# Sums of an attention through DRAM: one write and four reads of 256-byte runs, or two writes and four reads of 1024- and 1280-byte runs, in a new order of the instructions

## Chip, cores and metric

The kernel runs on one core of one Trainium2 chip. Its time is the device time of one execution in microseconds (us). A run's profile comes from one execution that the hardware profiler recorded, whose own device time is given beside the span from its first to its last instruction.

## What is computed

Causal attention with a decay, and on its result a gated projection. Eight batches, eight heads, 576 positions, 64 numbers a head:

```python
scores = q @ k.T / sqrt(64) + cum[:, None] - cum[None, :]      # cum: running sum of log(clip(f))
scores = where(j > i, -1e9, scores); scores -= scores.max(-1)
attn = exp(scores); attn = attn / (attn.sum(-1) + 1e-9)
x = attn @ v                                                   # heads side by side: 8 x 576 x 512
gate = sigmoid(sum_k conv_w[k] * x[position - 4 + k])          # five taps
out = (gate * (x @ w_val)) @ w_out
```

Inputs and outputs are float32, the weights of the projections are float64 and are decoded on the chip into two parts each.

## The kernel before

The 64 heads are worked off as 32 pairs, numbered i (four pairs to a batch). One pair's way through the engines:

- **Scores** (`plan_s`). The 576 queries are nine blocks of 64. In three groups (`SG`) TensorE multiplies keys with queries in quarters of the array and adds the decay by a product of a selector `pk` with a table `st` in bfloat16 (for pair 0, by a float32 product of `p1` with the running sum). VectorE adds the mask and takes the extreme (line 421), ScalarE takes the exponential and, beside it, the sum of each row into `zs` (line 425).
- **Transposes** (`plan_pt`). VectorE transposes the exponentials in 32 by 32 blocks into `T` (line 460). ScalarE or GpSimd copies half of `T` into `U`, and four DMAs (U copies, "U<-T") bring the other halves across partitions. U has two buffers.
- **Sums.** GpSimd or VectorE adds 1e-9 into `zr` (line 433), VectorE takes reciprocals and transposes them (lines 437 and 438) into `zt`: row 32a + b of it holds, for block b, the 32 numbers of part a (a = 0..3; parts 0 and 1 are one half of the partitions, 2 and 3 the other). One DMA writes them to a DRAM buffer `zd` of 128 x 32 (four buffers), and four DMAs read them back into `zb`, each to 64 partitions that all get the same numbers: one for each side (five or four blocks, `SIDES`) and half.
- **Product** (`plan_pv`). TensorE multiplies U with v ("U,vt"), in 54 small products. VectorE multiplies the result by `zb` into `x32` (line 517).
- **Gate and projections** (`plan_pv`, `plan_moe`). x is split in two parts, `xh` and `xl`, for fp32r products. The five taps run on ScalarE, GpSimd and VectorE; for the first two pairs (`NCV`) they run on TensorE instead, with diagonal matrices that line 534 makes ("x,tm"). After every fourth pair the batch goes through `Mv` (x by w_val), the gate (line 593), a split in `hh` and `hl`, `Mo` (by w_out), an eviction (lines 634 and 636) and a store.

At the start VectorE, ScalarE and GpSimd also decode the weights (`plan_w`, lines 693 to 709; `sh`, `sl`, `ot` are its buffers), and `split` makes the table `st`: three casts to bfloat16 with two subtractions between them (line 347).

**What sets the order.** No loop order is followed. `Plan.add` records each step with its dependences; `ORDER` is a compressed table of numbers that says which step comes next, on which of the engines that may do it, and which PSUM bank its result gets. `Plan.order` unpacks it. Every engine and the DMA queue of SyncE (SP), which issues nearly all transfers, then run their steps strictly in that order, and a step that waits holds what stands behind it on its engine.

```python
def load(cls, span, prio, out, in_, reads=(), writes=(), hold=0.57, early=False):
    return plan.add(cls, {"SP": hold, "ACT": hold} if early else {"SP": hold}, prio,
                    lambda e: (nc.sync if e == "SP" else nc.scalar).dma_start(out=out, in_=in_), reads, writes, dma=span)
```

`hold` and `span` are the planner's costs; the chip does not see them.

Of the kernel before, what the change touches and what calls it, by code (L numbers as in the profile page):

```python
# [15 lines left out]
P = 128  # L16
D = 64
S = 576
PAD = 64
W = PAD + S  # L20
NB = 4
L0 = NB * P
# [22 lines left out]
    "c-l>pc}!G!w#Vz<y0!0n)vf*3erw<N?beRI1kjfN`bSgpk_Pz$kVzDsL`o-7WD=mA1ZZB;(EcIlB!G4T=p+s8OB&=Qio8USKN@rrK_>y^4?$k?prmKstyKNaId#tGd(Q"  # L45
    "b?8V<ls;V$4bI4Q0lH;#LU<KZkgC+;qYgEn!yI1mWoD1Zl8CM*(~aILs=xD;*xJiu`Q7(f6N2tXaU5^fG00m)DTx{XT{Frb1E1d6~YSPK+@Zr~aTfw)iw)B!a?Ca4PPf"
    "%>5{xKp@lLLJl!H3D^ndgwmx2iyo$B+Nn6U?<cCO+t+X2_z=Epm}H-8il?k_Tb(V+DXkM7ZD?#0hXXkz;oP>gbrW=C=i3hJ$!`Xp}Zr!0}k<RM1)vPT!;1`h+rcAf};^"
    "iL@og&?h^WlH-I<L6seZj3*06S0y6-GxKEe`28hGJ6{3vr5jup(<XfaiV3D{)nj<|29snz(c@md6LYxOjiI0eHaBqmOz&_Fd2_bKgc1c|F2x)`pA};|Z@;>P%NlVxy-K"
    "4h=EQAQbLy(Xo;3DxEagA_|{s!nEbP-AfkQ^jaz)fJ3be-~o@{za;>;qTHT(FnWMH!<EQYtBvq&kWO9Hu-aE)!2v_-u%Tkq?P`L^^4L(n~3kU*Yhe21G$OxJ8+v)Kd!N"
    "CdvV2meNgL1uMWL*h*;v?-Qm76ND;omas|zs5_K(%3JUZnN3PjQ>4?(^W-$;A(_r@CO43W$nE4b^DeoAvOuW^TftxH{d9x`lTebAbQKgc&Vf{_gt|eWr0>!Z#t0o_R8U"  # L50
    "=vP5M54lnyeM=+pE$dXQ0Im>AWJ?+G8ld*riJ3S))NqlQUoyq4;r=1Jq^8qy9}MY2#i_!;sXd4YU~u}&_5Fn)=A0B(}i_-~k8#vAhglAD;dj1FcGbB5W+_(TRNt<2w;T"
    "g*=8EOUohPim${sOPEeR4R+Zx=b~)8>nlXF6IGqf!Rf+QOtNA<qinoC6t#;fHlY*W76;?Y9AG2PcR3l!^|@*7aL|3*dx@>)Jj@C<35{B3(#EnpQvHHhO)$-W3Mu6XkuC"
# [92 lines left out]
def tile_decay_attention_gated_mlp(  # L145
# [11 lines left out]
    B, H = out.shape[0], out.shape[2] // D  # L157
# [635 lines left out]
```

## Time and profile before

| | |
|---|---|
| median of 3 runs | 438.51 us (438.19 to 442.37) |
| the profiled execution | 437.04 us |
| its span, first to last instruction | 435.3 us |
| mean granted TensorE clock in it | 0.991 |

Busy times in a profile are unions of an engine's instructions. "PE" is TensorE's matmuls, "PEld" its weight loads, DVE VectorE, ACT ScalarE, POOL GpSimd, SP SyncE. In a list of waits or behind "<-" stands what released the waiting instruction last: an engine with tile and line, or a DMA. PEclk is the granted share of the full clock.

### The profile page before, as it was taken

The page shows a single profiled execution, that of the slowest core. Times are in us where ns is not written, and L with a number is a line of the kernel's source. Part 1 is how long each engine was busy: PE and PEld are TensorE (multiplying, and loading weights), DVE is VectorE, ACT ScalarE, POOL GpSimd, SP SyncE. Part 2 cuts the span into 40 slices and gives each one's busy share as a digit, 9 for nine tenths or more (in the row PEclk, how much of TensorE's full clock was granted, in tenths as well). Part 3 has the DMA queues.
Part 4 walks back from the last instruction along what each step waited for, and adds up shares of the span by engine and source line. Part 5 has one row for each costly group of instructions (what it writes and reads, how often), then busy time and mean ns, then how long its engine had stood idle before and what let it go on. Part 6 is the DMA issues. An engine that isn't in the chain of part 4 may idle for free.

```text
span 435.3 us, 16742 instructions
## 1 busy us (share of the span) xinstructions
PE 416.7 (96%) x6660; PEld 356.1 (82%) x6660; DVE 373.7 (86%) x1034; ACT 338.1 (78%) x840; POOL 287.9 (66%) x295
## 2 busy tenths in 40 slices
PE   7679899999999989999999999999999999999996
PEld 5456678888998878888898889887898888988885
DVE  6999889998999888898899987978999987997751
ACT  7899879998888869888777877667987988763430
POOL 4575847587959692898779475898675779752200
PEclk9899999999999999999999999999999999999999
DMA  7889987878777975977885677777867776387112
GB/s 286 291 213 240 239 233 196 223 206 210 216 202 199 253 199 152 256 211 200 220 249 143 184 212 206 197 209 216 243 174 209 223 184 191 74 205 224 57 46 98
DMA packets 74694, 86.93 MB, mean 200 GB/s; under 512 B 48120, under 2 KB 48120, under 8 KB 74616
## 3 DMA queue, kind: packets, MB, share of 16 engines
q1 hardware_dynamic: 74328, 85.28, 71.1%
q8 instruction: 52, 0.85, 0.8%
q10 hardware_dynamic: 288, 0.59, 0.4%
q14 instruction: 26, 0.21, 0.2%
HBM read 51.99 MB, written 10.26 MB: 143 GB/s over the span
## 4 chain that ended last, share of the span: by engine, by line
PE 88%; DVE 4%; DMA 3%; ACT 2%; issue 1%; POOL 1%; SPq 0%; POOLq 0%
PE banks L235 88%; DVE banks L421 2%; DMA U<-T 1%; DMA vt<-in_v_dram 1%; DVE T L460 1%; ACT P L425 1%; DMA cwu<-in_conv_w_dram 1%; POOL wall L709 1%; DVE negm L421 0%; ACT L334 0%; SPq L262 0%; POOL U L250 0%; DVE sh L707 0%; ACT sl L693 0%; ACT gate L333 0%
## 5 line engine op out<-in xcount | busy, mean ns | idle before, releaser
L425 ACT ACTIVATE P<-banks,negm 128x576 f32<-128x576 f32 (+8 forms) x288 | 150.0, 530 | 42.4 <-DVE negm L421 30.7
L421 DVE CUSTOM_DVE_ANT_0 banks<-banks,mk 128x576 f32<-128x576 f32 (+8 forms) x288 | 135.3, 508 | 15.2 <-PE banks L235 11.4
L562 POOL TENSOR_TENSOR gate<-gate,tm 128x576 f32<-128x576 f32 x77 | 109.7, 1425 | 33.6 <-DVE gate L560 12.0
L460 DVE STREAM_TRANSPOSE T<-P 128x1088 f32<-128x1088 f32 (+2 forms) x96 | 110.5, 1165 | 5.2 <-ACT P L425 2.8
L235 PE MATMUL banks<-xh,wall 128*128 128x288 f32 x512 | 107.1, 298 | 0.0
L235 PE MATMUL banks<-Xr 64*64 64x288 f32 (+8 forms) x1280 | 103.1, 410 | 1.4 <-DMA Xr<-in_x_dram 1.4
L235 PEld LDWEIGHTS banks<-U,vt 64*64 64x64 f32 x3456 | 91.8, 135 | 8.3 <-issue 3.1
L235 PE MATMUL banks<-U,vt 64*64 64x128 f32 (+1 forms) x3456 | 93.2, 256 | 3.8 <-issue 1.8
L235 PE MATMUL banks<-wall,hh 128*128 128x512 f32 x288 | 90.4, 395 | 0.0
L235 PEld LDWEIGHTS banks<-xh,wall 128*128 128x128 f32 x512 | 83.3, 188 | 4.2 <-issue 1.4
L235 PEld LDWEIGHTS banks<-Xr 64*64 64x64 f32 x1280 | 63.8, 134 | 16.5 <-issue 5.9
L235 PE MATMUL banks<-xl,wall 128*128 128x288 f32 x256 | 75.4, 295 | 0.0
L235 PEld LDWEIGHTS banks<-wall,hh 128*128 128x128 f32 x288 | 52.6, 188 | 13.0 <-issue 1.6
L425 ACT ACTIVATION_READ_ACCUMULATOR P<-banks,negm 128x1 f32 x288 | 58.7, 204 | 0.0
L250 ACT COPY U<-T 128x1440 f32<-128x1440 f32 x40 | 55.5, 1396 | 3.4 <-DVE T L460 1.7
L235 PE MATMUL banks<-wall,hl 128*128 128x512 f32 x144 | 56.2, 390 | 0.0
L235 PE MATMUL banks<-st,pk 64*64 64x448 bf16 (+8 forms) x620 | 45.8, 291 | 7.5 <-ACT st L250 3.7
L257 POOL TENSOR_SCALAR tm<-x,cw 128x576 f32<-128x576 f32 x40 | 30.1, 753 | 34.1 <-DVE gate L560 13.3
L235 PEld LDWEIGHTS banks<-xl,wall 128*128 128x128 f32 x256 | 48.0, 188 | 0.3
L607 POOL TENSOR_TENSOR hl<-h,hh 128x576 fp32r<-128x576 f32 (+2 forms) x34 | 34.4, 1027 | 12.6 <-DVE gate L560 4.1
L526 POOL TENSOR_TENSOR xl<-x,xh 128x576 fp32r<-128x576 f32 x25 | 35.6, 1430 | 10.6 <-DVE sl L695 4.9
L235 PEld LDWEIGHTS <-pk 64*64 64x64 bf16 x620 | 25.6, 106 | 20.0 <-issue 16.2
(104 smaller groups left out, 482.8 us busy)
## 6 DMA issues: line engine op xcount, KB each, us to landing
U<-T SPq DMA_DIRECT2D x128, 180.0 KB
Xr<-in_x_dram SPq DMA_DIRECT2D x63, 288.0 KB
vt<-in_v_dram SPq DMA_DIRECT2D x32, 320.0 KB
out_dram<-ot SPq DMA_DIRECT2D x36, 256.0 KB
vt<-in_v_dram SPq DMA_DIRECT2D x32, 256.0 KB
zb<-zd SPq DMA_DIRECT2D x64, 80.0 KB
zb<-zd SPq DMA_DIRECT2D x64, 64.0 KB
sl<-in_w_out_dram SPq DMA_DIRECT2D x2, 512.0 KB
```

The costliest lines, as they stand in the source:

```text
L235: nc.tensor.matmul(out, lhsT=lhsT, rhs=rhs, start=start, stop=stop)
L250: (eng.copy if eng is nc.scalar else eng.tensor_copy)(out=out, in_=in_)
L257: eng.tensor_scalar(out=out, in0=in_, scalar1=col, scalar2=0.0, op0=ALU.mult, op1=ALU.add)
L421: nc.vector.tensor_tensor_reduce(out=sl, in0=sl, in1=mk[:, S - ext:], op0=ALU.add, op1=ALU.min, scale=-0.125, scalar=3.0e38, accum_out=neg ...
L425: nc.scalar.activation(out=dst, in_=bank(key)[:, a0:a0 + ext], func=AF.Exp, bias=negm[r][:, col], scale=-1.0, accum_out=zs[r][:, col])
L460: nc.vector.transpose(out=bass.AP(Tt.tensor, Tt.offset + 32 * FB[js[0]], [pitch, (32, nk), (CW, 2), (1, 32)]), in_=Pt[u])
L526: any_("xl", {"POOL": 1.4, "DVE": 0.67}, p, lambda eng: eng.tensor_tensor(out=xl[s], in0=xv, in1=xh[s][:, :].bitcast(F32), op=ALU.subtract ...
L562: eng.tensor_tensor(out=gt, in0=gt, in1=to, op=ALU.add)
L607: eng.tensor_tensor(out=hl[jj][:, y:y + x1 - x0], in0=h2[jj % 2][:, x0:x1], in1=hh[jj][:, y:y + x1 - x0].bitcast(F32), op=ALU.subtract)
L709: any_(nm, {"POOL": 1.2, "DVE": DM / 960.0 + 0.075}, p, lambda eng, lo=lo, zz=zz, m=m: eng.tensor_tensor(out=lo, in0=zz, in1=m, op=ALU.mul ...
```

## The change

The 128 x 32 numbers of a pair are laid down in DRAM half by half: for each half n of the partitions, 64 numbers of block 0, 64 of block 1, and so on. Two writes, one for each half of `zt`, take the place of one. A read of w blocks of one half then finds its w x 64 numbers side by side, so its source is one run of 256 w bytes for each partition, and not w runs of 256 bytes that lie 512 bytes apart. Each read depends on the write of its own half. The numbers that reach `zb` are the same.

```diff
         zq = zd[i % 4]
-        to = bass.AP(zq.tensor, zq.offset, [(32, 4), (P, 32), (1, 32)])
-        load("zD", 0.4, p + 0.01, to, zt[r], [("zt", r)], [("zd", i % 4)], hold=0.48)
+        for n in range(2):
+            to = bass.AP(zq.tensor, zq.offset + 32 * D * n, [(32, 2), (D, 32), (1, 32)])
+            load("zD", 0.4, p + 0.01, to, zt[r][D * n:D * n + D], [("zt", r)], [("zd", i % 4, n)], hold=0.48)
         c = 0
         for y, half in enumerate(SIDES):
             w = len(half)
             for h in range(2):
                 load("zB", 0.4, p + 0.03, zb[r][D * h:D * h + D, D * c:D * (c + w)],
-                     bass.AP(zq.tensor, zq.offset + P * c + D * (h ^ y), [(0, D), (P, w), (1, D)]), [("zd", i % 4)], [("zb", r, y, h)], hold=0.48)
+                     bass.AP(zq.tensor, zq.offset + D * (32 * (h ^ y) + c), [(0, D), (1, D * w)]), [("zd", i % 4, h ^ y)], [("zb", r, y, h)], hold=0.48)
             c += w
```

The table is made anew (2386 steps for 2354), its first line:

```diff
 ORDER = (
-    "c-l>pc}!G!w#Vz<y0!0n)vf*3erw<N?beRI1kjfN`bSgpk_Pz$kVzDsL`o-7WD=mA1ZZB;(EcIlB!G4T=p+s8OB&=Qio8USKN@rrK_>y^4?$k?prmKstyKNaId#tGd(Q"
+    "c-l=;Sxi)Uy03F;-}mj*zE_>v_o`F-zBCV_JRmZOAP;RdlYq^GR&$dEc~E2$P#)-#n+W>QluQE1O@#3#4SEwnCINI3E$u{*hX$DhkVzDs<VsOJGgUd~eE)CxeZTMb{kK"
...
 )
```

So the order differs on every engine from the start. Three places follow.

ScalarE at the start, before: the decay table is `st_70`, its values before the cast are in `gate`, `P_80` to `P_82` are the exponentials of pair 0 and `sh`, `sl` the decoding.

```order
L697 ACTIVATE sl<-sl 128x512
L700 ACTIVATE sh<-sh 128x512
L697 ACTIVATE sh<-sh 128x512
L425 ACTIVATE P_80,zs_92<-banks,negm_90 128x512
L425 ACTIVATE P_81,zs_92<-banks,negm_90 128x448
L425 ACTIVATE P_81,zs_92<-banks,negm_90 128x192
L703 ACTIVATE sh<-sh,ebias 128x512
L425 ACTIVATE P_81,zs_92<-banks,negm_90 128x64
L700 ACTIVATE sl<-sl 128x512
L425 ACTIVATE P_81,zs_92<-banks,negm_90 128x320
L250 CAST st_70<-gate 128x576
```

The same place after (its lines count one more from the change on):

```order
L250 CAST st_70<-gate 128x576
L701 ACTIVATE sh<-sh 128x512
L698 ACTIVATE sh<-sh 128x512
L704 ACTIVATE sh<-sh,ebias 128x512
L425 ACTIVATE P_81,zs_92<-banks,negm_90 128x448
L425 ACTIVATE P_81,zs_92<-banks,negm_90 128x192
L250 CAST st_70<-gate 128x576
L425 ACTIVATE P_80,zs_92<-banks,negm_90 128x512
L425 ACTIVATE P_81,zs_92<-banks,negm_90 128x320
L425 ACTIVATE P_81,zs_92<-banks,negm_90 128x64
L250 CAST st_70<-gate 128x576
```

One cast stood on ScalarE before, all three stand there after, with three exponentials between the second and the third.

VectorE at the start, before, from the running sum `x_101` on:

```order
L336 SCALAR_TENSOR_TENSOR x_101<-one,gate 128x576
L338 TENSOR_SCALAR ref<-x_101 128x1
L701 TENSOR_SCALAR sl<-sl 128x512
L695 TENSOR_SCALAR sl<-sl 128x512
L695 TENSOR_SCALAR sh<-sh 128x512
L250 CAST st_70<-gate 128x576
L701 TENSOR_SCALAR sh<-sh 128x512
```

The same place after; `tm` is where the diagonal matrices of pair 0 go.

```order
L336 SCALAR_TENSOR_TENSOR x_101<-one,gate 128x576
L338 TENSOR_SCALAR ref<-x_101 128x1
L535 TENSOR_TENSOR tm<-ident,cw 128x640
L702 TENSOR_SCALAR sl<-sl 128x512
L696 TENSOR_SCALAR sh<-sh 128x512
L696 TENSOR_SCALAR sl<-sl 128x512
L702 TENSOR_SCALAR sh<-sh 128x512
```

The diagonal matrices, which GpSimd made before, are made here, and the first cast is gone to ScalarE (the second one too, further on).

SP at pair 2, before: `U_85` is the buffer of pairs 0 and 2, `zd_68` and `zb_98` are pair 2's sums.

```order
L262 DMA zd_68<-zt_96 4x32x32
L262 DMA Xr_78<-in_x_dram 128x576
L262 DMA U_85<-T_83 32x1440
L262 DMA vt_87<-in_v_dram 128x640
L262 DMA zb_98<-zd_68 64x4x64
L262 DMA Xr_76<-in_x_dram 128x576
L262 DMA U_85<-T_83 32x1440 x2
L262 DMA zb_98<-zd_68 64x5x64
L262 DMA U_85<-T_83 32x1440
```

The same place after:

```order
L262 DMA U_85<-T_83 32x1440
L262 DMA zb_99<-zd_67 64x256
L262 DMA U_85<-T_83 32x1440 x3
L262 DMA zd_68<-zt_96 2x32x32 x2
L262 DMA ot<-in_w_out_dram 128x1024
L262 DMA Xr_76<-in_x_dram 128x576
L262 DMA zb_98<-zd_68 64x320 x2
L262 DMA zb_98<-zd_68 64x256
```

The four U copies of pair 2 stood between the write and the reads of its sums; now they stand ahead of both writes, with one read of pair 1 between them.

On TensorE the convolution of pair 0 now stands ahead of the third group of scores of pair 3, not behind it, and the first half of the convolution of pair 1 behind the product of pair 2, not ahead of it.

## Rows read from the trace of the kernel before

**Rows 1.** Busy time by stage: start, length, then each engine, clock, DMA share, GB/s.
```profile
core 0: us, PE busy (x) PEld busy (x) DVE busy (x) ACT busy (x) POOL busy (x), PEclk, DMA share, GB/s
0.00:62.15 62.15, 49.67 (x768) 37.59 (x769) 54.30 (x164) 53.78 (x135) 38.27 (x64) 0.95 0.87 253
62.15:403.70 341.55, 338.97 (x5680) 293.57 (x5681) 302.79 (x838) 274.55 (x688) 246.80 (x229) 1.00 0.75 202
403.70:431.75 28.05, 28.02 (x213) 24.98 (x212) 16.64 (x33) 9.15 (x17) 2.87 (x2) 1.00 0.16 58
```

**Rows 2.** Waits of TensorE: for whom, us in total, times, longest us.
```profile
PE banks L235 <- ACT P L425: 4.2, 8, 1.0
PE banks L235 <- ACT st L250: 3.7, 1, 3.7
...
PE banks L235 <- DMA U<-T: 1.1, 1, 1.1
```

**Rows 3.** The chain that ended last, in order of time: start us, us, what.
```profile
46.37 5.02 DMA U<-T
...
51.52 10.24 PE banks L235 x125
...
62.15 95.26 PE banks L235 x1351
```

**Rows 4.** Timeline of TensorE, 24 to 62.5 us: start us, us, instructions.
```profile
32.03 0.70 PE L235 MATMUL banks<-st,pk 64*64 64x128 bf16 x6 [0.30 <-ACT P L425]
...
33.17 0.42 PE L235 MATMUL banks<-st,pk 64*64 64x288 bf16 x6
...
35.03 2.69 PE L235 MATMUL banks<-x,tm 128*128 128x288 f32 x10 [0.48 <-ACT P L425]
...
40.71 2.70 PE L235 MATMUL banks<-U,vt 64*64 64x128 f32 x105
...
51.52 4.34 PE L235 MATMUL banks<-U,vt 64*64 64x128 f32 x104 [1.12 <-DMA U<-T]
```

**Rows 5.** Busy time in 52.50 to 55.80 us; columns as in rows 1.
```profile
52.50:55.80 3.30, 3.30 (x78) 3.18 (x68) 1.28 (x2) 1.92 (x5) 0.97 (x2) 0.50 1.03 246
```

**Rows 6.** DMA packets of the whole run, from the page.
```profile
DMA packets 74694, 86.93 MB, mean 200 GB/s; under 512 B 48120, under 2 KB 48120, under 8 KB 74616
```

**Rows 7.** Tile zb: engines that sat idle before its instructions, until what.
```profile
  DMA zb<-zd: 1.5, 2
```

**Rows 8.** Issues of line 262 on SP: duration ns min/median/max, first and last start.
```profile
L262 SPq DMA_DIRECT2D zb<-zd x128: 573/622/1502, 25.0 to 400.8; - x128
...
L262 SPq DMA_DIRECT2D zd<-zt x32: 578/590/644, 22.1 to 393.2; - x32
```

**Rows 9.** Waits of SP: for whom, us in total, times, longest us.
```profile
SPq L262 <- DMA zd<-zt: 17.8, 15, 3.3
```

**Rows 10.** Timeline of VectorE and ScalarE at the start: start us, us, instructions.
```profile
8.51 0.52 DVE L250 CAST st<-gate 128x576 bf16<-128x576 f32 x1
...
13.62 0.81 DVE L347 SCALAR_TENSOR_TENSOR gate<-st,sel,gate 128x576 f32<-128x576 bf16 x1
...
14.74 0.67 ACT L250 CAST st<-gate 128x576 bf16<-128x576 f32 x1
...
32.14 0.93 DVE L517 TENSOR_TENSOR x<-banks,zb 128x256 f32<-128x256 f32 x3
```

**Rows 11.** Costliest groups, from the page: busy us, mean ns, idle before.
```profile
L425 ACT ACTIVATE P<-banks,negm 128x576 f32<-128x576 f32 (+8 forms) x288 | 150.0, 530 | 42.4 <-DVE negm L421 30.7
```

**Rows 12.** Groups by form: busy us, mean ns, idle before.
```profile
L460 DVE STREAM_TRANSPOSE T<-P 128x1024 f32<-128x1024 f32 x32 | 39.5, 1233 | 1.2 <-ACT P L425 1.1 <-DMA out_dram<-ot 0.2
...
L421 DVE CUSTOM_DVE_ANT_0 banks<-banks,mk 128x192 f32<-128x192 f32 x32 | 12.0, 379 | 0.9 <-PE banks L235 0.7
...
L526 DVE TENSOR_TENSOR xl<-x,xh 128x576 fp32r<-128x576 f32 x7 | 5.7, 823 | 0.0
...
L707 DVE TENSOR_SCALAR sh<-wall 128x512 int32<-128x512 int32 x4 | 1.6, 402 | 0.0
```

More of the change, by code (lines that the diff above doesn't have):

```diff
@@ L49 @@
[L49 to L52, printed above, removed]
@@ new lines @@
+    "*>-{z#wJ>^B7f+>BKZ)Td*w545olJV0thum_^JurW4zb5n_Huji4MDIqnSbJ+OqC!%Sc%z#?!Jm<Hy+XDBju0N;UY!XdaAE|06nwcv(;J!}K9AGeNqhhbrhI2c#L_23?"
+    "&?6`TL1dQQ^a0|d|%n`PLdx~GjZ{kTf0Rg~00G|QRQA^-9o{1X+>WGKvUF;Tck0QpZvAY-yb_9QbR}vhAPxx2(5n>q^C%nTw2Tj;7m_y7k-h~ZfK|+pTAovMH!VV6?-3"
+    "Qiz*T5DwiJil>)3$+eJc}?xTqI85zu<!45|ITS07Os-UdGPgKLK<22e@yEH?h6ge(V%>oVZRrO;CYz#1`-sae_EXImEret>9kZx@c`gG`NVL!=5F;U<JHEaDu;4e!@P%"
+    "QSf3s27iI@8}Smcmly-D6Wa+Kd>^5kprnG-0}6|DK<pw2Nd+(uULoGa{(|iUe*l-THwhq#MJ19x5q(rSev>##xJkT6cn2y;M$$Rb8N85cpc1K{D7#>iF-w>vJR&@#*h%"
@@ new lines @@
+    "%E10Sct_*UvV1;L*KUr{bnTS<$QX5v1Wqdq0X@DAz{<q4sS6eP8iCMk{hB&m+{kk$(xfv2eu`Yg2tzfRaBY*GL;6I~%}($;B<v<A{PL4m$TBhYVv_o?6D4`^hxgMO1XP"
+    "P;^XMf*fsqWwghpbe0|#bb$FqLMBke<m2wB;p9kPw&J#&=8SD*AQW14|SW?O)}7fj7G)`t&fyM50hp{Wl}36fc`+>utw42q(-uhETmtd+KB<;MaE0UHOAjabEHd*D~!j"
+    "aIDLi+GM7j>bO(8n@dN!Gshc)S>7$KO?@=F72dI5qB6FB}5&eX^MWwJndXC;qe?uK-oJL<lS4i(k=gB^@oIFLoOzx$}$s^={kRFonkS7>3jA1%V-elZl958yxXVDkXy^"
+    "P<eSJ3tJPmCqT9OEkbC&o781$BVlMqi=cqj%Bk80~a5Ym`1opQZPs3*?*VBhnZeAeYg4)--wny^KDhlF4xvNIRhBSZinptC6+NxWsB@{RRCRy@}pI=g4QsFUfmkCfUz="
@@ new lines @@
+    "Oa4f{$vVw?NWa305wDXkvKGl@@-6aDtR*sw>7;dY#jFN~iYB7{%=(5|$5$|y=`*YyaxZI<1yZiFmRLl}I?G3Cq^#2y>8F|FtP!q}_KG#fddd}0giJO?#2)8Pa5q_-TqP"
+    "Uit#fC%2V4O!MRV|8(YINzxZ7MM?>SjciSrtSFvZ18G8_2K!e(ZG_JQ?|o~H$wXK3eWpST9z9M{h?G256fHig~J>|%alsYNczc}kR$;}Ll|3WmMN-KG<1-OO+Kz5Gl3D"
+    "||HLH@=C@VY39Mc?bL?yN_ANHi@n=FH)}ag#s3jO}oJx;g2(K@@_KE@>+OzgyVcru+A?r=a`H98U6?QXF8WbW@s2h!6*J4Kge$8H?W7f5aa)t%S@Q@H)e&|$Zlod;}zJ"
+    "K*su5#%n5!AtxMW1ZJ_k=+Id}+F5VUP5`TkvlV28AgxA?h!LrcK*k=xKyLoN=2h364Bi?1oOZJbHJ+_T=og&~|Wxr*AWXm}|&JKH%4|Dc}AScf05WZ)AW)88Zg=@ljp;"
@@ new lines @@
+    "1sLnB{E<i5v)0Knp^E)gdB5PkBzkIl(0F2`?${7aj>)1?>U=8WI+TJ3=PZBfQJL&A!k6MRWmTbN+{27A>&Xd7HcnFULs=+Jr$tMFd0rq7BisXrBFyy(21$&Ty7RB~bw?"
+    "3HL>7qBV90r;#(o8Q~05&U3m14T2$2kEmTZEEo`U3odi+aLODzRNy@1^l}zCQPFkIkti=}5~2Bhf-w=3UoUDAjR-#T$b1o>AsdvA3vO|oVn5Uk%?Ogv0MrH5$s3?%=oh"
+    "I=6ciOiWx+Fnf^X!%<dmdt{+M)$^PGdocBGJOUWAB=;$f%{s)I%$vDhRQE0f|naap=7MfmH29bQHHTJTQrUI5FcrGS_t{>brh-*VQZ^U@7zOlFrUWILQADIh!KM7aVki"
+    "n}lUhd|Cf63hvDWoThucEBTY)#7$>gP6m8D>rb-!pDLg`H`HYI4>{AnTn#EBx@6Ml+9wX@D9{0@091b`|=+7JTwFK%Le6Tc^N9nJH+$yetEyRSA1T%00D{xd5k|TKZiO"
```

72 lines of the change are left out of this document (30 added, 42 removed).

## Prediction

> **What bounds the kernel now.** I read the busy time by stage first. The cut at 62.15 us is where TensorE stops waiting, the cut at 403.70 us is its last wait. In the long middle stage TensorE is busy 338.97 of 341.55 us, so only 2.58 us can be won there; in the first 62.15 us it is busy 49.67, so 12.48 us of waiting lie there; after 431.75 us come one eviction and its store, 435.3 - 431.75 = 3.55 us [rows 1]. The list of what TensorE waited for says the same in causes: 3.7 us once for the cast that makes the decay table, 4.2 us in eight short waits for exponentials, 1.1 us once for the copies into U. No row of it names zd or zb [rows 2]. The chain of work that ended last, in order of time, shows the end of the start: a U copy issued at 46.37 us takes 5.02 us, TensorE starts on it at 51.52, and from 62.15 us on the pieces of the chain are long ones of TensorE, such as 95.26 us [rows 3]. The timeline of TensorE puts prices on the start: the convolution of pair 0 begins at 35.03 us, a product (scores times values) takes 2.70 us, and the product that had waited 1.12 us for U takes 4.34 us [rows 4]. [...] So the kernel is bound by TensorE's own work from 62 us on, and before that by VectorE and by what VectorE feeds.
>
> **Part 1: runs of 1024 and 1280 bytes.** A pair reads its sums in four reads of 64 partitions by 5 or 4 pieces of 256 bytes: 64 x (5 + 5 + 4 + 4) = 1152 runs, 36,864 over 32 pairs, of the 74,694 packets of the page [rows 6]. After it is 4 x 64 = 256 runs a pair, 8,192 in all. That empties the transfer engines somewhat. It is worth nothing to the end as long as no engine on the path waits for zb, and VectorE waited for it twice, 1.5 us together [rows 7], while TensorE was fed all the same. I take 0; the bounds are -1.5 (both waits were on the path) and 0. The stores and the reads of U, x and v gain some room too; where that could count is only the copy of 5.02 us, and that is priced in part 3.
>
> [...]
>
> **Part 2: one more issue a pair on SP.** 32 writes become 64. One issue of zd takes 0.590 us and one of zb 0.622 us [rows 8], so SP carries 32 x 0.59 = 18.9 us more. SP issues some 14 transfers a pair (4 U copies, 4 zb reads, 4 loads of x and v, 1 zd write, 1 store), at about 0.6 us some 8.4 us of the 13.0 us that a pair takes on TensorE ((49.67 + 338.97 + 28.02) / 32, rows 1): there is room for a fifteenth. Where SP stands is the wait of a read for its write to land: 17.8 us over the run, 15 waits, at most 3.3 us [rows 9]. Each read now waits for one half only, but that half is issued up to one issue later. I take 0, since what SP issues is mostly wanted some us later; the bounds are -1.1, TensorE's whole wait for U, were SP to come to the copies sooner, and the price of the rival on SP below.
>
> **Part 3: the new order, at the start.** The instructions are the same but for the zd writes, so the new order is paid or repaid where TensorE waits: in the first 62 us.
>
> (a) The casts that build the decay table. Before, two of the first three run on VectorE and the third on ScalarE directly behind the second subtraction (13.62 + 0.81 = 14.43 us, cast at 14.74) [rows 10]. After, all three run on ScalarE and three exponentials stand between the second and the third. At a mean of 0.530 us [rows 11] they take 1.59 us beside a subtraction of 0.81: +0.8 us for the first decay product of pair 1. Bounds 0 and +1.6 (nothing hides them).
>
> (b) Pair 0's result x. VectorE now does more ahead of it: the diagonal matrices (no row shows them on VectorE; nearest is a 576-column two-operand instruction, 0.823 us), one more transpose, 1.233, two more bit operations, 0.80, and two short reductions of 64 and 192 columns, at most 0.379 each, 0.76 [rows 12]; two casts of 0.52 left [rows 10]. That is 0.82 + 1.23 + 0.80 + 0.76 - 1.04 = +2.57 us. x was ready at 32.14 + 0.93 = 33.07 us and TensorE came to it at 35.03, so 1.96 us of it are hidden. With half of (a) passed on to VectorE, x is ready at 33.07 + 2.57 + 0.4 = 36.04, a start 1.0 us later. TensorE has then also done one group of scores less, which comes behind the convolution now: 33.17 - 32.03 = 1.1 us [rows 4]. So TensorE is 1.0 + 1.1 = 2.1 us late there. Bounds 0 (VectorE's idle gaps swallow it) and +3.6 (nothing hidden beyond half).
>
> (c) The clock. A wait of one or two microseconds ahead of that convolution may bring a stretch at 0.50. Cost 0 or 1.64; I take +0.8.
>
> (d) The product of pair 2. After, its four U copies are issued almost together, one read between them, ahead of both zd writes; before, a zd write and a load stood ahead of them and four other transfers between them. Five issues fewer are 5 x 0.62 = 3.1 us: the last goes out at about 43.3 us and, landing 5.02 us later, is there at 48.3. The convolution of pair 1 also moves from before this product to behind its start, so TensorE arrives 2.69 us earlier in work: 51.52 - 1.12 - 2.69 + 2.1 = 49.8. The wait of 1.12 us and the cold 1.64 us go: -2.76. Late next is the convolution behind it, at 49.8 + 2.7 = 52.5 us, which needs x of pair 1; VectorE has more ahead of that x too. I have no row for how much of it counts, and leave it to the upper end of (b). Bounds -2.76 and 0.
>
> Start: 2.1 - 2.76 + 0.8 = +0.1 us ((a) is inside (b)).
>
> **Part 4: the rest.** In the middle the old order lost 2.58 us. Another order of the same work can at best save that; three more waits of the 1.12 us kind, one of them followed by a cold stretch, would cost 3 x 1.12 + 1.64 = 5.0. I take +0.3, as there is far more to lose than to win. The tail has the same last instructions (two halves of a row block, an eviction, a store): 0.
>
> **Sum.** 435.3 us of span + 0.1 + 0.3 = 435.7. The profiled execution took 437.04, 1.74 us around its span, which gives 437.4. The median of the runs shown is 438.51, 1.47 above that execution; so 438.9 us as a median. A measurement of this kernel tells about 1% from no change, 4.4 us: below 434.1 is faster, above 442.9 slower.
>
> **Rivals.**
> *No change within 1%*, the forecast: the reads were hidden, the order loses as much as it wins. For it: no wait for zb or zd on TensorE. Chance 0.64.
>
> *Faster: the emptier transfer engines and the new order close the start.* U copies and v loads land sooner, and the waits of the start shrink to the ones that no order removes. Of 12.48 us I can't see more than half go, since the cast's 3.7 us and the first loads stand at the head of every order: -6.2 and one cold stretch, -1.64: 438.5 - 7.8 = 430.7. For it: 5.02 us for a copy, far in excess of its issue. Against: the same VectorE work stands ahead of the same products, and (b) adds to it. Chance 0.17.
>
> *Slower: SP falls behind.* The mechanism: the second zd write and a slower landing hold SP at the first read of a pair, and the U copies queued behind it go out late. It decides from the point where a U copy lands after TensorE has come to its product, which happened once before. Each such product costs 1.12 + 1.64 = 2.76 us; at three more of them, 438.9 + 8.3 = 447.2. Against: in the middle of the trace it never happened. Chance 0.10.
>
> [...]
>
> *Slower: the new order is worse at the start or has bad places in the middle*: (b) at +3.6 with a cold stretch and (d) not coming, or 5.0 in the middle: 438.5 + 5.2 = 443.7. For it: the old order loses almost nothing in 341 us, and a new one can hardly do better. Chance 0.09.
>
> **How the numbers follow.** Faster 0.17, same 0.64, slower 0.10 + 0.09 = 0.19. The likeliest case is 438.9; its own range is 435 to 442.5 (start -2.8 to +3, middle -1 to +3). The range that is to hold 8 of 10 goes halfway into the faster case and into the milder slower one: 433.0 to 444.5.
>
> **What would show it.** Right: packets near 74,694 - 28,672 = 46,000 on the page and a lower transfer share, with TensorE busy about 417 us as before; a wait before the first convolution (start at 36 to 37 us) and none for U at pair 2; SP waiting for zd no less than 17.8 us. Wrong: the product of pair 2 again waiting for U, or more than 6 us of waits of TensorE between 62 and 404 us (slower); TensorE without waits from 45 us on (faster); VectorE waiting for zb in many pairs, which would make the reads a matter of the path after all.

## The result, and the profile after

| | before | after |
|---|---|---|
| median | 439.14 us (436.65 to 442.45) | 442.30 us (439.58 to 446.63) |
| the profiled execution | 437.04 us | 439.58 us |
| its span | 435.3 us | 437.8 us |

The ratio of after to before is 1.0069, 95% interval [1.004, 1.0097]: 0.7% slower, within the 1% that this kernel's measurement tells from no change, and inside the predicted range. The forecast was 438.9 us. Here and below a median counts every execution, while a ratio and its interval leave out those more than 1.5% above the fastest of their kernel, so the two need not agree.

The page of the kernel after, its TensorE line, its packets and SP's DMA queue (q1):

```profile
PE 418.6 (96%) x6660; PEld 357.1 (82%) x6660; DVE 374.0 (85%) x1032; ACT 336.6 (77%) x837; POOL 286.6 (65%) x299
...
DMA packets 46022, 86.93 MB, mean 199 GB/s; under 512 B 11256, under 2 KB 19448, under 8 KB 45944
...
q1 hardware_dynamic: 45512, 84.98, 67.9%
```

The wide reads are there: 46,022 packets and not 74,694 [rows 6]. By stage (columns as in [rows 1]):

```profile
0.00:62.15 62.15, 49.24 (x761) 37.19 (x762) 52.95 (x163) 52.43 (x135) 35.98 (x59) 0.92 0.76 230
62.15:404.00 341.85, 339.13 (x5647) 293.31 (x5649) 307.37 (x845) 273.93 (x684) 246.90 (x237) 1.00 0.73 206
404.00:434.20 30.20, 30.19 (x258) 26.64 (x258) 13.65 (x28) 9.66 (x18) 3.75 (x4) 1.00 0.15 54
```

The middle loses 341.85 - 339.13 = 2.72 us, where before lost 2.58. The start loses 62.15 - 49.24 = 12.91, where before lost 12.48. TensorE ends at 434.2 and not at 431.75. Of these 2.45 us, 0.4 are idle time of the start and 0.1 of the middle; the other 1.9 are busy time, 418.56 us and not 49.67 + 338.97 + 28.02 = 416.66; the clock of the start is 0.92 and not 0.95 (below). The product of pair 3 starts at 64.85 and not at 62.15 us, 2.70 later. Six projection products (from 63.76 us) stand ahead of it that before runs behind it, 1.09 us, so for equal work 1.6 of the 2.45 us are there by then. That the idle time of the start hardly grew hides that its waits have changed hands. What TensorE waited for in the kernel after (us in total, times, longest us):

```profile
PE banks L235 <- DMA Xr<-in_x_dram: 4.1, 1, 4.1
PE banks L235 <- ACT P L425: 3.4, 5, 1.2
PE banks L235 <- issue: 3.1, 3, 1.6
PE banks L352 <- ACT P L425: 2.0, 1, 2.0
...
PE banks L235 <- ACT st L250: 0.7, 1, 0.7
...
PE banks L235 <- DMA U<-T: 0.2, 1, 0.2
```

The 3.7 us for `st` are down to 0.7, the 1.1 us for U to 0.2 [rows 2]. The first row is new at this size: 4.1 us for `Xr`, pair 0's keys and queries, where before waited 1.4. The 2.0 us for `P` are new too: they stand at 17.70 us, just ahead of the wait for `st`, so the smaller wait for `st` is no gain, and the decay product of pair 1 starts at 19.06 and not at 15.46. The timeline of TensorE says where:

```profile
8.39 3.61 PE L235 MATMUL banks<-Xr 64*64 64x448 f32 x28 [4.15 <-DMA Xr<-in_x_dram]
...
17.70 0.66 PE L352 MATMUL banks<-ident 128*128 128x128 f32 x4 [1.97 <-ACT P L425]
19.06 0.64 PE L235 MATMUL banks<-st,pk 64*64 64x448 bf16 x8 [0.70 <-ACT st L250]
...
38.59 0.34 PE L235 MATMUL banks<-U,vt 64*64 64x64 f32 x6 [1.16 <-issue]
...
40.19 2.69 PE L235 MATMUL banks<-x,tm 128*128 128x288 f32 x10
...
52.38 3.25 PE L235 MATMUL banks<-U,vt 64*64 64x128 f32 x108
...
63.76 0.51 PE L235 MATMUL banks<-xh,wall 128*128 128x288 f32 x1
...
64.85 2.70 PE L235 MATMUL banks<-U,vt 64*64 64x128 f32 x105
```

The very first scores start at 8.39 us; in the trace of before they start at 5.59. The convolution of pair 0 starts at 40.19, not 35.03 [rows 4], and the product of pair 2, at 52.38, no longer waits.

Why the load is late stands in the first issues. ScalarE's queue in the kernel after, and SP's:

```profile
0.81 0.39 ACTq L262 DMA_DIRECT2D gate<-in_f_dram  x1
1.24 0.93 ACTq L262 DMA_DIRECT2D Xr<-in_x_dram  x2
```

```profile
0.79 0.39 SPq L262 DMA_DIRECT2D cwu<-in_conv_w_dram  x1
1.23 0.42 SPq L262 DMA_DIRECT2D sl<-in_w_out_dram  x1
1.69 0.43 SPq L262 DMA_DIRECT2D sh<-in_w_val_dram  x1
2.17 0.92 SPq L262 DMA_DIRECT2D Xr<-in_x_dram  x2
```

Pair 0's load has two halves of 288 KB. Before, one went out second on SP and one second on ScalarE. The new order puts both on ScalarE's queue, behind `f`, which makes three transfers there, and the two weight loads of 512 KB move up one place each on SP. The transfers of 5 to 7 us in the kernel after, by queue (q1 is SP's, q10 ScalarE's; packets, MB, share of the 16 engines):

```profile
q1 hardware_dynamic: 143, 0.51, 62.5%
q10 hardware_dynamic: 154, 0.32, 40.8%
```

The engines are full (62.5% + 40.8%), and 60% of their time goes to SP's queue, with its 1 MB of weights, while TensorE stands waiting for what is in ScalarE's queue. Both queues moved data in these two microseconds, 0.51 MB and 0.32 MB; how the engines chose between them is not shown.

### The profile page after: what moved, and what is told of

Its sections match the earlier page's. It is cut to its first block, busy times and chain, and to the rows that moved or that the text cites. A ratio compares the mean times of both kernels' runs of the same rounds, so it can differ in the third digit from the quotient of the medians.

```text
span 437.8 us, 16818 instructions
## 1 busy us (share of the span) xinstructions
PE 418.6 (96%) x6660; PEld 357.1 (82%) x6660; DVE 374.0 (85%) x1032; ACT 336.6 (77%) x837; POOL 286.6 (65%) x299
## 2 busy tenths in 40 slices
DMA packets 46022, 86.93 MB, mean 199 GB/s; under 512 B 11256, under 2 KB 19448, under 8 KB 45944
## 3 DMA queue, kind: packets, MB, share of 16 engines
q1 hardware_dynamic: 45512, 84.98, 67.9%
## 4 chain that ended last, share of the span: by engine, by line
PE 79%; DMA 3%; ACT 2%; POOL 1%; issue 1%; DVE 1%; SPq 1%; ACTq 0%; DVEq 0%
PE banks L235 79%; DMA U<-T 2%; ACT P L425 1%; DMA zb<-zd 1%; SPq L262 1%; ACT U L250 1%; DVE x L518 0%; POOL U L250 0%; POOL tm L535 0%; POOL sh L700 0%; POOL wall L710 0%; ACT ot L704 0%; ACT ot L635 0%; DVE sl L696 0%; DVE T L461 0%
## 5 line engine op out<-in xcount | busy, mean ns | idle before, releaser
L425 ACT ACTIVATE P<-banks,negm 128x320 f32<-128x320 f32 (+8 forms) x288 | 149.7, 528 | 49.7 <-DVE negm L421 36.5
L421 DVE CUSTOM_DVE_ANT_0 banks<-banks,mk 128x64 f32<-128x64 f32 (+8 forms) x288 | 135.3, 508 | 14.1 <-PE banks L235 13.0
L563 POOL TENSOR_TENSOR gate<-gate,tm 128x576 f32<-128x576 f32 x76 | 108.1, 1423 | 37.5 <-DVE xl L527 7.3
L235 PE MATMUL banks<-Xr 64*64 64x128 f32 (+8 forms) x1280 | 106.5, 418 | 5.7 <-DMA Xr<-in_x_dram 4.1
L235 PE MATMUL banks<-U,vt 64*64 64x128 f32 (+1 forms) x3456 | 91.9, 254 | 1.4 <-issue 1.2
L235 PEld LDWEIGHTS banks<-Xr 64*64 64x64 f32 x1280 | 65.9, 137 | 21.8 <-issue 13.3
L250 ACT COPY U<-T 128x1440 f32<-128x1440 f32 x43 | 60.1, 1399 | 4.5 <-PE banks L235 3.0
L235 PE MATMUL banks<-st,pk 64*64 64x288 bf16 (+7 forms) x620 | 45.9, 292 | 4.6 <-ACT P L425 3.4
L608 POOL TENSOR_TENSOR hl<-h,hh 128x576 fp32r<-128x576 f32 (+2 forms) x37 | 37.3, 1024 | 10.2 <-DVE hl L608 4.7
L527 POOL TENSOR_TENSOR xl<-x,xh 128x576 fp32r<-128x576 f32 x24 | 34.2, 1425 | 13.3 <-DVE xh L250 6.8
L235 PEld LDWEIGHTS <-pk 64*64 64x64 bf16 x620 | 25.7, 106 | 18.5 <-issue 14.3
```

Of the source, the lines that this page charges most:

```text
L235: nc.tensor.matmul(out, lhsT=lhsT, rhs=rhs, start=start, stop=stop)
L250: (eng.copy if eng is nc.scalar else eng.tensor_copy)(out=out, in_=in_)
L421: nc.vector.tensor_tensor_reduce(out=sl, in0=sl, in1=mk[:, S - ext:], op0=ALU.add, op1=ALU.min, scale=-0.125, scalar=3.0e38, accum_out=neg ...
L425: nc.scalar.activation(out=dst, in_=bank(key)[:, a0:a0 + ext], func=AF.Exp, bias=negm[r][:, col], scale=-1.0, accum_out=zs[r][:, col])
L527: any_("xl", {"POOL": 1.4, "DVE": 0.67}, p, lambda eng: eng.tensor_tensor(out=xl[s], in0=xv, in1=xh[s][:, :].bitcast(F32), op=ALU.subtract ...
L563: eng.tensor_tensor(out=gt, in0=gt, in1=to, op=ALU.add)
```

## The experiments

An experiment is the kernel before or after with a few steps of `Plan.order` moved, or with the data layout of the other. "First scores" is their start on TensorE; "product of pair 3" is the start of the piece at which the middle begins (62.15 us in before). In the order of after six projection products, 1.09 us, stand ahead of that piece, so this column compares kernels of one order, not of two.

| kernel | first scores, us | product of pair 3, us | median, us | ratio to before |
|---|---|---|---|---|
| before | 5.59 | 62.15 | 439.14 | |
| after | 8.39 | 64.85 | 442.30 | 1.0069 [1.004, 1.0097] |
| 1 after, early load | 6.16 | 62.25 | 438.24 | 0.9969 [0.9935, 1.0003] |
| 1 again | 5.33 | 63.60 | 440.69 | 1.0051 [1.0017, 1.0086] |
| 2 before, late load | 8.30 | 64.97 | 444.48 | 1.0060 [1.0019, 1.0101] |
| 3 after, load later still | 11.01 | 68.79 | 443.84 | 1.0116 [1.0051, 1.0181] |
| 4 before, new layout | 5.49 | 65.29 | 442.58 | 1.0037 [1.0002, 1.0071] |
| 5 before, two writes, old layout | 5.53 | 64.18 | 442.50 | 1.0103 [1.005, 1.0156] |
| 6 before, second write late | 5.43 | 70.22 | 483.02 | 1.1014 [1.0963, 1.1066] |
| 7 after, old layout | 8.40 | 64.69 | 443.59 | 1.0090 [1.0054, 1.0125] |
| 8 after, early load, old layout | 5.55 | 62.12 | 439.13 | 1.0014 [0.9979, 1.0049] |
| 9 after, early load, two writes, old layout | 5.79 | 62.69 | 439.95 | 1.0056 [1.0017, 1.0095] |
| 10 after, early load, casts moved | 5.67 | 64.80 | 440.96 | 1.0023 [0.9984, 1.0061] |
| 11 after, early load, pair 4's load earlier | 5.47 | 62.69 | 439.16 | 1.0036 [1.0, 1.0072] |

One caution ahead of all: the two rows 1 are the same kernel on two chips. Their medians lie 0.6% apart and their intervals don't meet. So one difference below about 0.8% between two of these kernels decides nothing; what decides is the trace, and whether many kernels fall on the same side. The chips differ between other rows too; each ratio is to runs of before on the same chip.

### The load of pair 0 (1, 2, 3)

1: the kernel after, with the first half of pair 0's load second on SP, as before.

```diff
+        load = [w for w in steps if w >> 3 == 5][0]
+        steps.remove(load)
+        steps.insert([w >> 3 for w in steps].index(28) + 1, load - load % 8 + 4)
```

> The kernel after, with one load moved: the first half of pair 0's q and k goes out as the second transfer of SP, as in the kernel before, and not as the third of ScalarE's queue. Theory 1 (the late load): TensorE's wait for that load falls from 4.1 us to about 1.4, the stretch of the clock at 0.50 that begins near 8 us goes, and the span falls from 437.8 by 2.5 to 4 us; the ratio to the kernel before is 0.998 to 1.002. Theory 2 (the layout with its two writes): nothing changes, ratio 1.007. Theory 3 (the rest of the new order: casts, diagonal matrices, more work ahead of pair 0's x): the load is early but the later waits grow by as much, ratio 1.005 to 1.007.

Timeline of TensorE in this kernel:

```profile
6.16 3.58 PE L243 MATMUL banks<-Xr 64*64 64x448 f32 x28 [1.92 <-DMA Xr<-in_x_dram]
...
36.50 2.69 PE L243 MATMUL banks<-x,tm 128*128 128x288 f32 x10
...
41.08 1.09 PE L243 MATMUL banks<-Xr 64*64 64x448 f32 x16 [1.54 <-DMA Xr<-in_x_dram]
```

The first scores are 2.2 us earlier than in the kernel after, the convolution 3.7, the product of pair 3 2.6. The wait for the load is 1.92 us and not 1.4, the span 435.9, so 1.9 us shorter and not 2.5 to 4. The slow stretch of the clock went, by the granted clock, 1.00 in 6.20 to 9.60 us, but the pace did not change with it: the same 28 score products took 3.61 us in the kernel after, at a granted clock of 0.50, and 3.58 here. The queues in 5 to 7 us:

```profile
q1 hardware_dynamic: 216, 0.81, 98.8%
q10 hardware_dynamic: 7, 0.01, 1.5%
```

ScalarE's queue is through by then. The same kernel once more:

> The kernel after with the first half of pair 0's load back on SP, a second time, beside the two above on one chip. Theory T1 (the load is what the change lost): ratio to before below 1.000 again, 0.995 to 0.999, so the order and the layout without that move are no loss. Rival (the first ratio of 0.9969 was chance and the rest of the new order is worth nothing): 1.000 to 1.004.

```profile
5.33 2.06 PE L243 MATMUL banks<-Xr 64*64 64x448 f32 x28 [1.10 <-DMA Xr<-in_x_dram]
...
35.28 2.69 PE L243 MATMUL banks<-x,tm 128*128 128x288 f32 x10
...
40.96 1.09 PE L243 MATMUL banks<-Xr 64*64 64x448 f32 x16 [2.65 <-DMA Xr<-in_x_dram]
```

The start was better still, but at 40.96 us pair 4's scores waited 2.65 us for their load, 1.1 more than the first time. The 28 scores took 2.06 us this time. The ratio, 1.0051, is even above the rival's range: an order that is mended at the start is no gain over before, and on this chip it is a small loss. Both medians are below that of the kernel after, but this ratio alone can't be told from its 1.0069.

2: the order of before, with that half put behind the other on ScalarE's queue.

> The kernel before, with that one load moved to where the kernel after has it, third on ScalarE's queue. Theory 1: the first scores start near 8.4 us and not 5.6, and the ratio to the kernel before is 1.005 to 1.009. Theories 2 and 3: ratio 0.999 to 1.002, since the decay table, ready at 15.4 us, is waited for anyway.

```profile
8.30 3.79 PE L243 MATMUL banks<-Xr 64*64 64x288 f32 x26 [4.07 <-DMA Xr<-in_x_dram]
...
39.88 4.32 PE L243 MATMUL banks<-x,tm 128*128 128x288 f32 x16
```

The one move gives the old order the late start: first scores at 8.30, convolution at 39.88, and a ratio of 1.0060 [1.0019, 1.0101], as theory 1 had it: 2.6 us on the same chip. (The medians, 444.48 against 439.74, would give 4.7. The last row here, and that of kernel 3, ends with the window shown, at 44 us.)

3: the suspected cost made larger. The half stands eighth on SP, behind a small load, both weight loads and the four halves of pairs 1 and 2 (the recorded text says sixth).

```diff
+        for node in (186, 187, 239, 240, 5):
+            word = [w for w in steps if w >> 3 == node][0]
+            steps.remove(word)
+            steps.insert([w >> 3 for w in steps].index(135), word - word % 8 + 4)
```

> The kernel after with the first half of pair 0's load later still: sixth in SP's queue, behind both weight loads and the four halves of pairs 1 and 2. Some 2.5 MB stand in that queue up to its end; at the 0.4 MB per us that the transfer engines move from 5.3 us on in the kernel with the early load, it is there at about 10.6 us and the first scores start at about 11.2 us, 2.8 us later than in the kernel after (8.39). Theory T1 (every microsecond that the first scores come late is one at the end): 442.3 + 2.8 = 445.1 us, ratio to before 1.012 to 1.016, the scores of pair 1 at about 21.9 and the convolution of pair 0 at about 43. Rival (the late load is swallowed by other waits at the start, and what the change lost is chance or lies elsewhere): those two starts shift by less than 1.5 us, ratio 1.004 to 1.009 as with the kernel after.

```profile
11.01 3.89 PE L244 MATMUL banks<-Xr 64*64 64x448 f32 x28 [6.77 <-DMA Xr<-in_x_dram]
...
42.45 1.72 PE L244 MATMUL banks<-x,tm 128*128 128x288 f32 x6
```

First scores at 11.01 (11.2 expected), convolution at 42.45 (43), ratio 1.0116 [1.0051, 1.0181], just under what was expected; 2.6 us more of waiting brought 1.5 us more of median, 0.5% by ratio. Taken together: six rows of the table have the new order with the load early, and their ratios are 0.9969 to 1.0056, 1.0025 in the mean; the two with it late have 1.0069 and 1.0090, 1.0080 in the mean; the one with it later still 1.0116. No early one reaches a late one, though neighbours' intervals overlap. By these means the late load costs 0.55%, 2.4 us, and by kernel 2 2.6 us: most of the 0.69% of the result. Whether the rest of the new order costs something too stays open, since on the chip of the second kernel 1 all three early kernels (the second 1, 9 and 11) are 0.4 to 0.6% above before.

### The place of the second write on SP (4, 5, 6)

4: the order of before with the new layout, the second write right behind the first.

```diff
+        steps = [x for w in steps for x in ((w, w + 8) if w >> 3 in first else (w,))]
```

> The kernel before in its own order, with the new layout alone: the second write stands directly behind the first on SP, the reads take runs of 1024 and 1280 bytes. Theories 1 and 3: ratio 0.998 to 1.002, packets 46,022, SP waiting for zd no more than 17.8 us. Theory 2: ratio 1.005 or more, with SP's waits for zd longer than 17.8 us and waits of TensorE for U.

TensorE's waits and its timeline:

```profile
PE banks L245 <- DMA U<-T: 5.6, 4, 2.8
```

```profile
53.58 0.44 PE L245 MATMUL banks<-U,vt 64*64 64x128 f32 x4 [2.79 <-DMA U<-T]
```

In the old order the second write stands ahead of U copies at the start, where the transfer engines are crowded (a DMA share of 0.84 in the first 62 us of this kernel). The wait for U at pair 2's product grows from 1.12 [rows 4] to 2.79 us, and the product of pair 3 starts 3.1 us later. The ratio, 1.0037, lies between the two expectations; theory 2's waits for U came, its longer waits of SP for zd did not (8.5 us, not more than 17.8).

5: the same with the old layout, so that the reads are of 256 bytes again.

```diff
+        for n in range(2):
+            to = bass.AP(zq.tensor, zq.offset + D * n, [(32, 2), (P, 32), (1, 32)])
```

> The order of before, two writes right behind each other as in the run before last of this order, but the old layout in DRAM: the reads take pieces of 256 bytes again. Theory A (the extra issue ahead of the U copies costs): as with the wide layout, waits for U of 4 to 6 us and a ratio of 1.003 to 1.005. Theory B (the wide layout costs, or saves transfer time): the ratio differs from 1.0037 by 0.003 or more; with narrow reads that crowd the queues it would be 1.006 to 1.008, with wide reads as the culprit 1.000. Packets about 74,700.

```profile
PE banks L245 <- DMA U<-T: 4.4, 5, 2.6
```

The waits for U are there too, so they come with the second write and not from the wide layout. The ratio, 1.0103, lies above both ranges, and further from 1.0037 than theory B asked. Its interval meets that of kernel 4, and the medians are alike (442.50, 442.58); whether narrow reads make it worse stays open.

6: as 4, but the half that is read second is written just ahead of its first read.

```diff
+            out += [held.pop(d) for d in sorted(self.nodes[n]["deps"] & set(held))]
+            out.append(w)
```

> The order of before with the new layout and its two writes; the half that is read first is written at the old place, the other one just ahead of its first read and no longer right behind the first. Theory A (the place on SP costs: the second issue stood ahead of the U copies at 23 and 34 us): the wait for U at pair 2's product goes back from 2.8 us to about 1.1, TensorE's waits for U from 5.6 to under 2 us, ratio 0.999 to 1.002. Theory B (the wide layout or the number of issues costs, wherever they stand): waits for U of 4 us or more stay, ratio 1.003 to 1.005.

Both theories missed: 483.02 us. SP's waits, and TensorE's:

```profile
SPq L284 <- DMA zd<-zt: 94.0, 49, 4.6
```

```profile
PE banks L257 <- DMA U<-T: 27.3, 13, 4.3
```

One case, first SP's timeline, then TensorE's:

```profile
50.25 0.55 SPq L284 DMA_DIRECT2D zd<-zt  x1
54.84 0.50 SPq L284 DMA_DIRECT2D zb<-zd  x1
55.38 0.59 SPq L284 DMA_DIRECT2D U<-T  x1
```

```profile
59.46 2.88 PE L257 MATMUL banks<-U,vt 64*64 64x128 f32 x54 [4.29 <-DMA U<-T]
```

The write is issued at 50.25. The read behind it holds SP until the write has landed, 4.0 us after the issue ended; a U copy behind the read goes out at 55.38, and TensorE waits 4.29 us for it. The edit was meant to clear the U copies of one issue and put a round trip through DRAM in front of them instead. This is the mechanism of the rival "SP falls behind", at its full price, 44 us.

### The layout in the new order (7, 8, 9)

7: the order of after with the old layout, one write at the place of the first of the two.

> The kernel after in its own order, with the old layout: one write of zd, where the first of the two stood, and reads of 256-byte runs. Theories 1 and 3: the ratio to the kernel before stays at 1.005 to 1.009, and packets are 74,694. Theory 2: ratio 0.999 to 1.002.

8: the same with the early load.

> The kernel after with the first half of pair 0's load back on SP and the old layout: one write, reads of 256 bytes. Theory T1 (the load is what lost the time, the layout is worth nothing): ratio to before 0.995 to 0.999, first scores at about 6.2 us, as with the wide layout. Theory T2 (the wide reads and two writes are worth something once the start is mended): 1.001 or more, so at least 0.4% above the run with the wide layout (0.9969), and more waiting of TensorE for DMA between 20 and 60 us.

9: the early load, two writes, reads of 256 bytes.

> The kernel after with the first half of pair 0's load back on SP, two writes, but the old layout in DRAM, so that the reads take pieces of 256 bytes; instruction for instruction the same order as the next kernel. Theory W (wide reads are worth some tenths of a per cent, as the pair with the order of before showed, 1.0037 with wide and 1.0103 with narrow reads): a ratio 0.003 to 0.006 above that of the kernel with wide reads, more waiting of TensorE for U or Xr. Theory N (the reads are hidden, that pair was chance): within 0.002. Packets about 74,700.

Kernels 7 and 8 are the second test of the load, with the old layout: the late start and the loss are there without the change of the layout (8.40 us, 1.0090 [1.0054, 1.0125]) and go when the load is early (5.55 us, 1.0014 [0.9979, 1.0049]); the intervals, from two chips, don't meet, and the product of pair 3 is 2.6 us earlier. So the loss comes with the order.

With the late load the medians are 442.30 wide and 443.59 narrow; with the early load 438.24 and 440.69 wide, 439.13 and 439.95 narrow. Kernel 9 and the second of kernels 1 ran on one chip and differ only in the width of the reads: 1.0056 [1.0017, 1.0095] and 1.0051 [1.0017, 1.0086]. That is theory N: within 0.002. Kernel 8 lies above T1's range; T2 would have read a gain of the wide reads into 1.0014 against 0.9969, but TensorE waited no longer for DMA between 20 and 60 us (1.4 us, 1.5 in the first kernel 1), and the second 1.0051 takes that gain away. No gain and no loss of the layout can be told here.

### Can the new order be made better than before? (10, 11)

10: the early load; the second subtraction, the third cast and pair 4's first half moved ahead by a few places.

```diff
+        move(173, 150)
+        move(174, 144)
+        move(403, 461)
```

> The kernel after with the first half of pair 0's load back on SP, the second subtraction (VectorE) and the third cast (ScalarE) each one to two places earlier, and one half of pair 4's load on SP ahead of pair 5's. Theory T1 (the change's loss is waiting at the start, and each wait at the start passes on to the end): the first scores start at about 6.2 us, the wait for st of 0.7 us goes and the decay product of pair 1 starts at about 16.2 and not at 16.8, the wait of 1.5 us for Xr at 41 us goes; a ratio to before of 0.993 to 0.996. Rival (waits of under a microsecond in the start are swallowed by the next wait, for x of pair 0 or for exponentials): those waits move and their sum falls by less than 0.5 us; ratio 0.997 as with the load alone.

The ratio, 1.0023 [0.9984, 1.0061], is above both ranges. The waits did as the rival said: the wait for Xr at 39 us went, another of 1.75 us that the profile puts to nothing came at 37.92 us, and the decay product started at 17.33, not 16.2, now with a wait of 0.74 us for exponentials, which had been pushed back. 11 has the last of the three moves alone:

> The kernel after with the first half of pair 0's load back on SP (as in the first of these experiments), and pair 4's first half issued on SP ahead of pair 5's, about 2 us earlier; no cast is moved. Theory T1 (a wait on the path from the start to 62 us costs its own length in the end): TensorE's wait of 1.5 us for Xr at 39.5 us goes, product of pair 3 about 1.5 us earlier, ratio to before 0.993 to 0.996, and below that of the same kernel without this edit in the same batch. Rival (the next wait, for exponentials or x, takes its place): the wait turns up within the next 10 us under another name, and the two ratios are within 0.002.

The wait for Xr went and waits for exponentials of 0.94 and 0.37 us stand at 41 and 42 us: again the rival. The ratio is 1.0036 [1.0, 1.0072], 0.0015 from that of the second kernel 1 on the same chip. I found no version that beats before.

## Why the prediction was right, point by point

**The class and the sum.** The forecast of no change within 1% came true, with 0.6 us left to its mark for slower, 442.9; the time was 3.4 us low. The reads were hidden, as forecast, but the order did not win what it lost. The sum had +0.4 us of span, and the profiled executions differ by 2.5. A term of 8.39 - 5.59 = 2.8 us is missing. Luck has a part in the total: the convolution of pair 0 comes 5.16 us late where the sum had 1.0, and from there to the product of pair 3 the kernel after takes 24.66 us where before took 27.12, with 2.2 us more of work in it (a group of scores, 1.1, and the six projection products, 1.09). So more was lost at the start than the sum had, and more won behind it.

**The step that failed** is the sentence that "the first loads stand at the head of every order". They do, but the new order moves one half of pair 0's load to another queue, third in it. The prediction counted VectorE's, ScalarE's and SP's steps around the change and did not list which transfer of the start stood on which of the two queues. Kernel 2 shows that this move alone makes the delay (first scores at 8.30 us for 5.59), kernel 3 that it grows with the place in the queue (11.01 for 8.39). The other half of that sentence, the cast's 3.7 us, fell to 0.7, but the decay product behind it came no earlier (19.06 us, 15.46 before).

**Part 1, 0 us: right.** VectorE's waits for zb in tile zb's view, which were 1.5 us [rows 7]:

```profile
  DMA zb<-zd: 1.9, 2
```

Packets came out as worked out, 46,022.

**Part 2, 0 us: right here, and for a reason of place.** I expected SP to wait for zd no less than the 17.8 us of [rows 9]. It waits less:

```profile
SPq L262 <- DMA zd<-zt: 6.7, 6, 1.3
```

What counts is what stands between a write and its read. In the kernel after it is two U copies for pair 0 (zd, zd, U, U, then the first read) and two loads for pair 2, so a write lands while SP issues something else. The new order does this with one write too (6.5 us in kernel 7, 4.7 in kernel 8), and in the old order the second write itself stands there (8.5 and 9.4 us, kernels 4 and 5). But in the old order the same second issue made TensorE wait 5.6 and 4.4 us for U (kernels 4 and 5), and with the read next to its write SP loses 94 us (kernel 6). What the extra write costs is a matter of its place: what stands between it and its read, and what waits behind it.

**Part 3 (a), +0.8 us.** From the first scores to the decay product of pair 1, before takes 15.46 - 5.59 = 9.87 us and after 19.06 - 8.39 = 10.67: +0.80. In other kernels of the new order with the casts in place it takes from 9.9 to 11.3 (the second of kernels 1, and 3), and the pace of the first scores is mixed into it: they took 3.61 us at a granted clock of 0.50 in the kernel after, and a like group of 26 took 2.00 in before, at 1.00. So +0.80 lies within the bounds, and the size of (a) is not shown.

**Part 3 (b), a start of 36.04 us.** Measured 40.19. Where the load is early the convolution starts at 36.50 and 35.28 (kernel 1 twice), 36.38 (8) and 36.54 (11), but at 38.01 in kernel 9 and at 39.51 in kernel 10, which had the wait of 1.75 us: in four of six the term was about right, on a start that the kernel after did not have. Of the 4.15 us too much, 2.8 are the load and 1.16 the wait at 38.59, which the profile puts to nothing.

**Part 3 (c) and (d).** (d) came true: no wait at 52.38, and none in the first of kernels 1, where TensorE is at this product at 50.03 us, near the 49.8 of the sum. The clock in four stretches of the kernel after (columns as in [rows 1]; the last but two numbers are the DMA share and GB/s, ahead of them the clock):

```profile
8.20:11.50 3.30, 3.11 (x26) 1.92 (x30) 1.28 (x4) 2.91 (x6) 0.88 (x6) 0.50 0.90 277
18.45:21.75 3.30, 2.69 (x35) 2.25 (x38) 3.27 (x8) 3.30 (x12) 2.46 (x3) 0.50 0.50 141
32.10:35.40 3.30, 3.30 (x45) 2.66 (x44) 3.27 (x9) 3.27 (x9) 2.27 (x2) 0.50 0.85 230
52.40:55.80 3.40, 3.40 (x114) 3.16 (x109) 3.37 (x14) 3.27 (x7) 3.23 (x4) 1.00 0.85 282
```

The stretch at half clock behind pair 2's product [rows 5] is gone, as (d) had it, but three others stand at the start, each after TensorE had waited: 4.15 us ahead of the first, 1.97 ahead of the second, which begins in a wait of 0.70, and 1.16 ahead of the third. Not every wait has one behind it: after that of 1.16 us at 38.59 the clock was 1.00 (38.60 to 41.90 us). Before had two, from 14.95 and from 52.50 us. The 1.64 us of the sum, its cold stretch, are 4.34 - 2.70, two products of before [rows 4], the longer one with a clock of 0.50 from 52.50 us on [rows 5]; that a stretch costs as much elsewhere was the author's estimate. One stretch more is the upper end of (c), 1.64 us, and by that estimate most of the 1.9 us that TensorE is busy longer. It is not shown to be the late load's doing: the second of kernels 1, with the load early, has three as well:

```profile
14.95:18.25 3.30, 3.00 (x38) 2.58 (x41) 3.27 (x10) 3.30 (x12) 2.45 (x3) 0.50 1.04 371
28.60:31.90 3.30, 3.06 (x43) 2.31 (x40) 3.27 (x9) 3.15 (x9) 2.28 (x2) 0.50 0.82 197
42.25:45.55 3.30, 3.30 (x17) 1.96 (x10) 3.23 (x15) 3.30 (x8) 0.29 (x1) 0.50 0.66 180
```

**Part 4.** The middle: +0.3 expected, 2.72 - 2.58 = +0.1 measured. The tail: 434.20 to 437.8 is 3.6 us, as before.

**The rivals.** "Faster" did not come: 12.91 us of waiting in the first 62 us, where it needed half. "The new order is worse" gave 443.7 us, nearer to the time measured than the forecast. Half of it came, a late convolution and one slow stretch more, but 2.8 us of the delay are the load and not VectorE's work; the other half did not: (d) came and the middle kept its 2.7 us. "SP falls behind" did not come in this order (6.7 us of waits for zd) and is real in others (94.0, kernel 6); that half a write lands more slowly than a whole one is not shown by itself.

**What stays open.** What TensorE waited for at 38.59 us; whether narrow reads cost something in the old order (kernels 4 and 5); and how much of the 0.7% is the rest of the new order, or another chip would not show, since kernel 1 moved by 0.6% between two.

## What to carry to other kernels

Write down for every transfer of the first microseconds which queue it stands in, at which place, and how many bytes of every queue are ahead of it or beside it: here a queue that shared full transfer engines with a megabyte of weights made an input 2.8 us late that was issued before 2.2 us. The write that is read back through DRAM wanted other work between itself and its read on the issuing queue: SP waited 94.0 us for zd without it (kernel 6), 8.5 with it (kernel 4). What such a write cost here was the wait in that place, and what its issue held up behind it: TensorE's waits for U, 27.3 and 5.6 us in these two kernels, 1.1 in before. And where one kernel on two chips differs by 0.6%, a difference of that size is argued from the trace and from several kernels on one side, not from one ratio.

## What was not expected of the hardware

With the second write of 8 KB of each pair put right ahead of its read, SP waited 94.0 us in 49 waits for such writes to land, 1.9 us each and up to 4.6 (kernel 6). In before, with writes of 16 KB, it was 17.8 us in 15 waits, 1.2 each and up to 3.3 [rows 9].

Runs of 1024 and 1280 bytes moved through the transfer engines at 22 to 23 bytes per ns and those of 256 at 14, by the medians of all packet records of the two traces (46 and 55 ns, against 18); by the means (60 and 72 ns, against 18.5) it is 17 to 18, against 14. All reads of zb together took 683 us of packet time before and 541 after, 142 us over 16 engines: 8.9 us of each, 2% of the span. So a count of packets that falls by 38% emptied the engines little (SP's queue went from 71.1% to 67.9% of them), for the same 86.93 MB.
